# Three V steps to a block instead of two, in a kernel that mixes attention and a Fourier layer on one core

## The chip, the core and the metric

The kernel runs on one core of a Trainium2 chip. A core has a matrix engine (PE, with its weight loads shown apart as PEld), a vector engine (DVE), an activation engine (ACT), a general engine (POOL) and an engine that here issues all DMAs (SP). The engines run side by side, each through its own list of instructions in order, and wait for each other by semaphores. The metric is the device time of one execution in microseconds.

## What is computed

```python
x = A_x                                            # 2048 tokens, 640 wide
g = sigmoid((x * gate_w).sum(-1, keepdims=True))
a = x @ dft_hid_re.T ;  b = x @ dft_hid_im.T       # DFT along the width
y = dft_seq_re @ a - dft_seq_im @ b                # DFT along the sequence
q = x @ wq (32 heads of 20) ; k = x @ wk ; v = x @ wv   # one k and v for all heads
o = softmax(q k^T / sqrt(20)) v, heads side by side, @ wo
out = g * y + (1 - g) * o
```

All inputs are float32 and filled matrices; nothing uses that the DFT matrices are regular.

## The kernel before

After a first stage (q, k, v, gate) nearly the whole time goes to one long loop in which PE works on two things in turn.

**Attention.** Heads go in pairs. In one pair the two heads use the two halves of PE's rows (partitions 0 to 63 and 64 to 127), so that two matmuls run at once, one in each half. For each pair and each half of the queries (index v, 0 to 31) there are three kinds of unit:

- an `a` unit (`a_unit`, L243): scores of 128 queries against 512 keys, of which DVE takes the maximum (L258). After 64 of them for one v, `a_reduce` and `a_final` (L260, L265) form the 62nd and 61st row of that v's query tile `qs`: the negated maximum, as a high and a low part. They go out to `m_d` and back into `qs` by two DMAs each, put into the program one and five ticks later. There are four query tiles (L141).
- a `b` unit (`b_unit`, L944): scores of 128 keys against 512 queries with the maximum taken off, and on ACT the exponential, into a tile `pt` (16 of them, L582). Four `b` units are one step.
- a `V` step (`av_step`, L961): four products of `pt` with the values. Here the four column groups of PE work at once, each over all 128 rows. 16 steps end one v; then `finish_half` (L968) starts a chain of DMAs and a reciprocal (`finish_sums`) for the row sums.

There are 512 steps in all. The scores go to five PSUM banks, S0 to S4, each of which is free again when DVE or ACT has read it.

**Fourier layer.** It is cut into products of 64 rows by 128 columns with 320 columns of data, in float32 made of a high and a low part. `y_put` queues pairs of products, `y0` and `y1` run one in each row half (`Halves`, L758). They serve first the DFT along the width (stage AB, begun ahead of the loop), then 112 chunks of 24 pairs for the sequence (stage Y), then the output projection (`oo`). For each chunk POOL adds two input blocks where a product asks for it (L522), rounds to the high part `ch` (L527) and subtracts for the low part `cl` (L528). Two chunks end one group of sums: `y_evict` (the words `E0`, `E1`) lets ACT copy the two PSUM tiles and POOL add them (L809), and `y_out` adds them to earlier parts.

**The order.** PE, ACT, DVE and POOL run in the order of the program text; the order of the DMAs on SP is chosen by the framework's planner. The loop goes over 256 rounds (`ROUNDS`, L1064) of two steps. Each round has a plan, a list of words: `b0S1` is a b unit of row half 0 into bank S1, `a1S3` an a unit of row half 1, `y0`/`y1` a Fourier product, `V` a V step. All plans with `V` have two of them at their end, one behind the other:

```python
    AB15 = (   # 8 b, 8 a, 15 pairs y, E0 E1 V V     56 + 16 rounds
    Y16 = (    # 8 b, 8 a, 16 pairs y, E0 E1 V V     168 rounds, stage Y
    Y12 = (    # 8 b, 8 a, 12 pairs y, E0 E1 V V     while a units are left
    N12 = (    # 8 b, 12 pairs y, E0 E1 V V
    N0 =       # 8 b, V V                            last two rounds
```

(The comments stand for the words.) The V words of a round take the steps of the round before (`old`); the first round has no V steps, and four follow the last one (L1119). A chunk of 24 pairs takes one round and a half. `later` (L227) puts DMAs and small work into the program a number of ticks afterwards; two ticks pass with each step. Work of `chores` (`a_final`, `finish_sums`, `scale_kept`) goes to DVE's list at the next V.

**The end.** `load_last` (L701) is called after round 252 (counted from 0; the 13th of the 14 rounds of Y12 and N12): POOL clears two tiles, ten DMAs fill them, and three DVE instructions (`scale_kept`, L712) make operands of them. After the last V step `finish_last` (L990) copies its result half on ACT and half on DVE (L995, L996), takes the reciprocal of the sums and feeds the last projections (`o_group`).

Of the kernel before, what the change touches and what calls it, by code (L numbers as in the profile page):

```python
# [23 lines left out]
NT = S // P  # L24
NPAIR = H // 2
LAST = NPAIR - 1
HALF = D // 2
SJ = NT // 2
# [5 lines left out]
def kernel(  # L34
# [24 lines left out]
    def bank(tag, name):  # L59
        if tag in BANKS:  # L60
            turn[tag] += 1
            tag = BANKS[tag][(turn[tag] - 1) % len(BANKS[tag])]
        return psum.tile([P, ROW], F32, tag=tag, name=name, bufs=1)
# [49 lines left out]
    def move(dst, src):  # L113
        nc.sync.dma_start(words(dst), words(src))  # L114
# [112 lines left out]
    def later(n, f, *args):  # L227
        todo.append((clock["n"] + n, f, args))

    def tick():  # L230
        clock["n"] += 1
        due = [t for t in todo if t[0] <= clock["n"]]
        todo[:] = [t for t in todo if t[0] > clock["n"]]
        for _, f, args in due:
            f(*args)
# [48 lines left out]
    def do_chores():  # L284
        for q in (chores, act_chores):
            while q:
                f, *args = q.pop(0)
                f(*args)

    NA = NPAIR * 64  # L290
    state = [0, 0]

    def a_half(hh, tag="A"):
        u = state[hh]
        if u >= NA:
            return
        a_unit(u, hh, tag)
        state[hh] = u + 1
        if state[1 - hh] <= u:
            return  # L300
        v, r = divmod(u, UV)
        if r == 8 and v + 1 < 2 * NPAIR:
            load_qs(v + 1)
        if r == UV - 1:
            chores.append((a_reduce, v))
            chores.append((a_final, v))
            if not stage["loop"]:
                do_chores()
# [180 lines left out]
    def a_src(i, th):  # L489
        return lambda r, sh: (cre, cim)[i][SJ * th + r, sh]  # L490

    def s_src(k):
        return lambda r, sh: s_d[k][r, sh].rearrange("p (j t) -> p j t", j=SJ)

    PRODUCTS = (
        ("p1", (a_src(0, 0),), None, None, None),
        ("p2", (a_src(1, 0),), None, None, None),
        ("p5", (a_src(0, 1), a_src(1, 1)), ALU.add, 1, t_d[1]),
        ("p6", (s_src(1), a_src(0, 0)), ALU.subtract, 2, t_d[2]),
        ("p7", (a_src(0, 0), a_src(0, 1)), ALU.subtract, None, t_d[3]),  # L500
        ("p3", (a_src(1, 0), s_src(2)), ALU.subtract, None, b_d[1, 1]),
        ("p4", (a_src(1, 1),), None, None, t_d[4]),
    )
# [216 lines left out]
    def load_late():  # L720
        tb = NT - 1
        t = acc[tb] = abp.tile([P, 2, HALF], F32, tag=f"ab0{tb}", name="acc")
        move(t, y_d[tb * P : (tb + 1) * P].rearrange("p (e n) -> p e n", e=2))
        later(4, lambda: nc.gpsimd.tensor_scalar(t, t, gate[:, tb : tb + 1], None, op0=ALU.mult))
# [211 lines left out]
    def y_put(n):  # L936

        while n > 0:
            n -= next(ys)[1]
# [4 lines left out]
    def b_unit(p, hh, kc, qc, tag="B"):  # L944
        b = 64 * hh
        ps = bank(tag, f"b_{p}_{kc}_{qc}_{hh}")
        nc.tensor.matmul(  # L947
            ps,
            ks[b : b + 62, kc * P : (kc + 1) * P],
            qs[NPAIR * (qc // 2) + p][b : b + 62, (qc % 2) * ROW : (qc % 2 + 1) * ROW],  # L950
            start=True,
            stop=True,
        )
        t = pp.tile([P, ROW], F32, name="pt")
        nc.scalar.activation(t, ps, AF.Exp, scale=SCALE)  # L955
        pt[(hh, kc, qc)] = t

    def av_mm(ps, g, t, kc, first, last):
        nc.tensor.matmul(ps[32 * g : 32 * g + 32, :], vsb[:, kc, :], t, start=first, stop=last)  # L959

    def av_step(p, qh, kc):  # L961
        if kc == 0:
            av[qh] = bank("V", f"av_{p}_{qh}")
        for hh in range(2):
            for j in range(2):
                av_mm(av[qh], 2 * hh + j, pt.pop((hh, kc, 2 * qh + j)), kc, kc == 0, kc == NT - 1)

    def finish_half(p, qh):  # L968
        ob = op.tile([P, ROW], F32, name="ob")
        nc.scalar.activation(ob, av[qh], AF.Copy)  # L970

        sm = op.tile([P, 16], F32, name="sm")
        n = (1, 3, 5) if (p, qh) == (LAST - 1, 1) else (2, 6, 10)
        later(n[0], move, sum_d[p, qh].rearrange("h (j t) -> (h j) t", j=2), ob.rearrange("(g r) t -> g r t", r=32)[:, DH])
        for hh in range(2):
            h = 2 * p + hh
            for j in range(2):
                js = slice((2 * qh + j) * ROW, (2 * qh + j + 1) * ROW)
                g = 32 * (2 * hh + j)
                later(n[0], move, oT_d[h * DH : (h + 1) * DH, js], ob[g : g + DH])  # L980
        later(n[1], move, sm, sum_d[p, qh].rearrange("h (s t) -> (h s) t", t=16))
        later(n[2], chores.append, (finish_sums, p, qh, sm))
# [28 lines left out]
    def scale_rows(p, qh):  # L1011
# [11 lines left out]
    AB15 = (  # L1023
        "b0S1 a1S3 b1S2 y0 y0 a1S0 y0 y0 y1 y0 y1 y0 b1S4 y0 a1S1 y0 b0S3 y1 y1 y0 y1 a0S2 y1 y0 b1S0 y0 y1 "
        "a0S4 y1 b0S1 y1 y1 a0S3 y1 y0 y1 y0 y1 y0 y1 y0 y1 b0S0 b1S2 a0S4 a1S1 E0 E1 V V"
    ).split()

    Y16 = (
        "b0S1 a1S0 a0S3 b1S4 y0 y1 y0 y1 y0 y1 y0 y1 y0 b1S2 y0 a1S1 y0 y0 a1S0 y0 b1S4 y0 y0 y1 y0 b1S3 y0 y1 "
        "a0S2 y1 b0S1 y1 y1 y0 y1 y0 y1 b0S4 y1 a0S0 y1 y1 b0S3 y1 a0S2 y1 a1S1 y0 E0 E1 V V"  # L1030
    ).split()

    Y12 = (
        "b0S0 a1S3 a0S4 y1 y1 b0S1 y1 y0 b1S2 y1 y0 y0 a1S0 b0S3 y1 y0 y1 y0 a1S1 y0 y0 b1S4 y0 y1 y0 a1S2 "
        "b0S0 y0 y1 y1 a0S3 y1 b1S4 a0S1 y0 y1 y1 y0 b1S2 a0S0 E0 E1 V V"
    ).split()

    N12 = (
        "b0S4 b1S2 b0S3 b1S0 b1S1 y0 y0 y1 y0 y1 y0 y1 y0 y1 y0 y1 y0 y1 y0 y1 y0 y1 y0 y1 y0 y1 y0 y1 "
        "b0S2 y1 b0S3 b1S4 E0 E1 V V"  # L1040
    ).split()


    N0 = [w for w in N12 if w[0] not in "yE"]

    LEAD = 12
    NL = 2 * (UV + LEAD)
    KL = 15 * SJ
# [12 lines left out]
                y_evict(g)  # L1061
    stage["loop"] = True

    ROUNDS = [(p, qh, kk) for qh in range(2) for p in range(NPAIR) for kk in range(NT // 2)]  # L1064
    NAB = 7 * SJ
    NY = 3 * SJ * len(PRODUCTS)

    NO = len(ROUNDS) - NT * 2

    def plan_of(n):  # L1070
        if n < NAB or NO <= n < NO + NT:
            return AB15
        if n < NAB + NY:
            return Y16
        if n >= len(ROUNDS) - 2:
            return N0
        return Y12 if state[1] < NA else N12

    old = []

    for rnd in ROUNDS:
        p, qh, kk = rnd
        nb, fed = [0, 0], False
        new = [(p, qh, 2 * kk), (p, qh, 2 * kk + 1)]
        plan = plan_of(ROUNDS.index(rnd))
        puts = plan.count("y0")
        for what in plan:
            if what == "V":
                if old:
                    st = old.pop(0)  # L1090
                    av_step(*st)
                    do_chores()
                    if st[2] == NT - 1 and st[:2] != (LAST, 1):
                        finish_half(*st[:2])
                continue
            g = int(what[1])
            if what[0] == "y":
                if not fed:
                    y_put(puts)
                    fed = True  # L1100
                halves.run(g)
            elif what[0] == "E":
                y_evict(g)
            elif what[0] == "b":
                b_unit(p, g, 2 * kk + nb[g] // 2, 2 * qh + nb[g] % 2, what[2:])
                if sum(nb) % 2 == 0:
                    tick()
                nb[g] += 1
            else:
                a_half(g, what[2:])  # L1110
        old += new
        if (p, qh, kk) == (LAST, 1, 4):
            load_last()
        if (p, qh, kk) == (LAST, 1, 5):
            load_late()
    for g in range(2):
        y_evict(g)

    for st in old:  # L1119
        av_step(*st)  # L1120
    finish_last()
    for e in range(2):
        begin_late(e)
# [49 lines left out]
```

## Time and profile before

| | |
|---|---|
| device time, median of 3 runs | 1738.46 us (1738.17 to 1738.92) |
| the profiled execution | 1739.45 us, its span 1737.7 us |
| PE busy | 1715.7 us, 99% of the span |
| DVE, ACT, POOL busy | 79%, 73%, 63% |
| granted PE clock | 0.996 of full speed |
| matmul instructions | 16752, of them 4096 for V steps (eight to a step) |

A busy matrix engine is read with care: matmuls overlap one another, in each row half and at their ends, so 99% busy says that something was always under way, and not that it could not be denser. What one kind of work costs is read from the distance between starts, not from the duration of one instruction.

### The profile page before, as it was taken

The numbers are of one execution on the slowest core, as the hardware profiler recorded it, in microseconds if no ns is written. First come the engines' busy times: TensorE is split into PE (matmuls) and PEld (weight loads), VectorE is DVE, ScalarE is ACT, GpSimd is POOL, SyncE is SP. The second block draws the span as 40 slices with busy tenths as digits, with TensorE's granted clock in tenths as the row PEclk, the third lists the DMA queues.
The fourth block names the chain that finished last, engine by engine and source line by source line (L and its number), as shares of the span: only waits on it lengthen the run. The fifth ranks groups of instructions, "written<-read, shape, count | busy, mean of one in ns | idle before, by whom it ended". The sixth has DMA issues, their size and how long they took to land.

```text
span 1737.7 us, 43681 instructions
## 1 busy us (share of the span) xinstructions
PE 1715.7 (99%) x16752; PEld 1223.3 (70%) x16752; DVE 1369.1 (79%) x2290; ACT 1261.7 (73%) x2543; POOL 1102.2 (63%) x921
## 2 busy tenths in 40 slices
PE   8999999999999999999999999999999999999997
PEld 6687777777777777777777777777777777777664
DVE  4788888888888888888888888888888888888813
ACT  4237888888777777777777777777777767788895
POOL 3045556333366568668777888888877765557784
PEclk9999999999999999999999999999999999999999
DMA  8552223222265546546666777555555533244332
GB/s 264 158 165 63 71 81 102 78 72 74 78 213 171 176 157 188 185 128 227 225 204 214 222 253 220 185 179 185 183 163 170 159 114 100 76 124 116 104 94 78
DMA packets 181502, 261.50 MB, mean 150 GB/s; under 512 B 35696, under 2 KB 136304, under 8 KB 181292
## 3 DMA queue, kind: packets, MB, share of 16 engines
q1 hardware_dynamic: 181292, 258.70, 47.1%
q8 instruction: 132, 2.16, 0.5%
q14 instruction: 78, 0.64, 0.1%
HBM read 184.42 MB, written 76.99 MB: 150 GB/s over the span
## 4 chain that ended last, share of the span: by engine, by line
PE 94%; DVE 2%; DMA 2%; issue 1%; ACT 1%; POOL 0%; SPq 0%; POOLq 0%; ACTq 0%; DVEq 0%
PE av L959 27%; PE y_p L767 20%; PE b L947 19%; PE a L251 15%; PE ab L767 7%; PE oo L767 3%; PE q L122 1%; DVE mx L258 1%; PE q L123 1%; PE q L124 1%; DMA wraw<-in_wq_dram 1%; DMA wraw<-in_wiT_dram 0%; ACT pt L955 0%; SPq L114 0%; DVE xl L361 0%
## 5 line engine op out<-in xcount | busy, mean ns | idle before, releaser
L258 DVE TENSOR_REDUCE mx<-a 128x1 f32<-128x512 f32 x2048 | 1282.7, 685 | 263.2 <-PE a L251 245.0
L955 ACT ACTIVATE pt<-b 128x512 f32<-128x512 f32 x2048 | 1068.9, 606 | 342.1 <-PE a L251 287.2
L947 PE MATMUL b<-qs,ks 62*128 62x512 f32 x2048 | 749.9, 408 | 3.8 <-DVE mx L258 1.8
L251 PE MATMUL a<-ks,qs 60*128 60x512 f32 x2048 | 702.0, 408 | 2.2 <-DVE mx L258 2.2
L767 PE MATMUL y_p<-tb,ch 64*128 64x320 f32 x3584 | 627.3, 306 | 0.0
L947 PEld LDWEIGHTS b<-qs,ks 62*128 62x128 f32 x2048 | 342.8, 185 | 220.8 <-DVE mx L258 155.1
L959 PE MATMUL av<-pt,vsb 128*32 128x512 f32 x4096 | 492.3, 598 | 0.0
L767 PEld LDWEIGHTS y_p<-tb,ch 64*128 64x128 f32 x3584 | 476.2, 185 | 9.8
L767 PE MATMUL y_p<-tb,cl 64*128 64x320 f32 x1792 | 442.4, 306 | 0.0
L251 PEld LDWEIGHTS a<-ks,qs 60*128 60x128 f32 x2048 | 345.8, 185 | 8.2 <-issue 4.0
L767 PEld LDWEIGHTS y_p<-tb,cl 64*128 64x128 f32 x1792 | 271.2, 185 | 5.1
L528 POOL TENSOR_TENSOR cl<-craw,ch 128x1024 fp32r<-128x1024 f32 x112 | 268.3, 2395 | 9.0
L959 PEld LDWEIGHTS av<-pt,vsb 128*32 128x32 f32 x4096 | 106.9, 109 | 226.1 <-issue 216.9
L809 POOL TENSOR_TENSOR yt<-yt,yu 128x320 f32<-128x320 f32 x86 | 74.9, 871 | 299.1 <-ACT yu L804 267.1
L809 POOL TENSOR_TENSOR abt<-abt,abu 128x320 f32<-128x320 f32 x64 | 55.7, 871 | 194.1 <-ACT abu L804 186.3
L522 POOL TENSOR_TENSOR craw<-craw 128x1024 f32<-128x1024 f32 x64 | 153.7, 2401 | 0.0
L527 POOL CAST ch<-craw 128x1024 fp32r<-128x1024 f32 x112 | 116.4, 1039 | 6.4 <-PE ab L767 2.3
L767 PE MATMUL oo<-wo,osp 64*128 64x320 f32 x816 | 92.6, 306 | 0.0
L767 PEld LDWEIGHTS oo<-wo,osp 64*128 64x128 f32 x816 | 87.4, 185 | 1.6
L554 POOL TENSOR_TENSOR tb<-braw,tb 128x320 fp32r<-128x320 f32 x80 | 68.5, 879 | 0.0
L767 PE MATMUL ab<-wbh,xh 64*128 64x320 f32 x256 | 60.1, 307 | 0.0
L767 PE MATMUL ab<-wbh,xl 64*128 64x320 f32 x256 | 59.8, 305 | 0.0
(138 smaller groups left out, 1626.9 us busy)
## 6 DMA issues: line engine op xcount, KB each, us to landing
craw<-in_cre_dram SPq DMA_DIRECT2D x80, 512.0 KB
craw<-in_cim_dram SPq DMA_DIRECT2D x64, 512.0 KB
s_d<-craw SPq DMA_DIRECT2D x32, 512.0 KB
craw<-s_d SPq DMA_DIRECT2D x32, 512.0 KB
braw<-b_d SPq DMA_DIRECT2D x80, 160.0 KB
xraw<-in_xT_dram SPq DMA_DIRECT2D x32, 320.0 KB
b_d<-abt SPq DMA_DIRECT2D x64, 160.0 KB
t_d<-braw SPq DMA_DIRECT2D x64, 160.0 KB
```

The lines of the kernel that those rows point to most:

```text
L122: nc.tensor.matmul(ps, wh, xh, start=(i == 0), stop=False)
L251: nc.tensor.matmul(ps, qs[v][b : b + 60, qb * P : (qb + 1) * P], ks[b : b + 60, c * ROW : (c + 1) * ROW], start=True, stop=True,)
L258: nc.vector.tensor_reduce(mx[v][:, hh, qb, c : c + 1], ps, axis=AX.X, op=ALU.max)
L522: nc.gpsimd.tensor_tensor(raw[0], raw[0], raw[1], op=how)
L527: nc.gpsimd.tensor_copy(h, raw[0])
L528: nc.gpsimd.tensor_tensor(l, raw[0], h.bitcast(F32), op=ALU.subtract)
L554: nc.gpsimd.tensor_tensor(t[:, 1], raw, t[:, 0].bitcast(F32), op=ALU.subtract)
L767: nc.tensor.matmul(ps, w, x, start=start, stop=stop)
L809: nc.gpsimd.tensor_tensor(t0, t0, t1, op=ALU.add)
L947: nc.tensor.matmul(ps, ks[b : b + 62, kc * P : (kc + 1) * P], qs[NPAIR * (qc // 2) + p][b : b + 62, (qc % 2) * ROW : (qc % 2 + 1) * ROW], ...
L955: nc.scalar.activation(t, ps, AF.Exp, scale=SCALE)
L959: nc.tensor.matmul(ps[32 * g : 32 * g + 32, :], vsb[:, kc, :], t, start=first, stop=last)
```

## The change

A plan Y24 is added: 12 b units, 12 a units, 24 pairs of products, E0 E1 and three V steps. In stage Y the 168 rounds of Y16 give way to seven cycles of 18 plans: each cycle has 12 of Y24, in couples, and 6 of Y16, in threes, so that a couple of Y24 (48 pairs) and three Y16 (48 pairs) each end one group of sums. The V words take steps from a list to which the plan's own steps are added before its words are run, so that V runs one step behind the newest one, and no longer two to four. The first plan, FIRST, has four more b units (one more step) and two V steps. The last two plans are N0 and a short one with four b units and two V steps, and no V steps follow the loop. `load_last` and `load_late` are called by the number of steps made. The other plans have the same words as before.

```diff
+    Y24 = (
+        "b1S0 a0S2 b1S4 y0 y0 a1S1 y0 y1 y0 b1S3 y0 y0 y1 y0 y1 a0S0 b1S2 y0 y1 y0 b1S4 y0 a1S1 y0 y0 y1 b0S3 y1 "
+        "y1 y0 a1S0 y0 b0S2 y1 y0 y1 y1 b0S4 a1S1 y0 y0 y1 y0 y1 y1 b0S3 y1 a0S0 y1 b0S2 y1 y1 y0 y1 a0S4 b1S1 y0 "
+        "y1 y0 y1 y0 y1 y0 y1 y0 y1 b0S2 a1S0 a0S3 y1 a1S4 a0S1 E0 E1 V V V"
+    ).split()
+
+    FIRST = AB15[:-2] + "b0S3 b1S0 b0S2 b1S3 V V".split()
...
-    ROUNDS = [(p, qh, kk) for qh in range(2) for p in range(NPAIR) for kk in range(NT // 2)]
+    STEPS = [(p, qh, kc) for qh in range(2) for p in range(NPAIR) for kc in range(NT)]
...
+    CYCLE = []
+    for k in range(8):
+        CYCLE += [Y16] * 3 if k in (2, 5) else [Y24] * 2
+
+    def plans():
+        yield FIRST
+        yield from [AB15] * (NAB - 1)
+        for _ in range(7):
+            yield from CYCLE
+        yield from [AB15] * NT
+        for _ in range(NT - 2):
+            yield Y12 if state[1] < NA else N12
+        yield N0
+        yield N0[:4] + N0[-2:]
...
-    for rnd in ROUNDS:
-        p, qh, kk = rnd
+    for plan in plans():
+        n = sum(w[0] == "b" for w in plan) // 4
+        new = STEPS[made : made + n]
+        made += n
+        old += new
...
             if what == "V":
-                if old:
-                    st = old.pop(0)
-                    av_step(*st)
-                    do_chores()
...
+                st = old.pop(0)
+                av_step(*st)
+                do_chores()
...
-        old += new
-        if (p, qh, kk) == (LAST, 1, 4):
+        if made == len(STEPS) - 5:
             load_last()
-        if (p, qh, kk) == (LAST, 1, 5):
+        if made == len(STEPS) - 3:
             load_late()
...
-    for st in old:
-        av_step(*st)
     finish_last()
```

More of the change, by code (lines that the diff above doesn't have):

```diff
@@ L1062 @@
     stage["loop"] = True
-    ROUNDS = [(p, qh, kk) for qh in range(2) for p in range(NPAIR) for kk in range(NT // 2)]
+    STEPS = [(p, qh, kc) for qh in range(2) for p in range(NPAIR) for kc in range(NT)]
     NAB = 7 * SJ
[L1066 to L1077, printed above, removed]
-    old = []
-    for rnd in ROUNDS:
-        p, qh, kk = rnd
+    CYCLE = []
[11 more added lines that the diff above has]
+        yield N0[:4] + N0[-2:]
+    made = 0
+    old = []
+    for plan in plans():
[3 more added lines that the diff above has]
+        old += new
         nb, fed = [0, 0], False
-        new = [(p, qh, 2 * kk), (p, qh, 2 * kk + 1)]
-        plan = plan_of(ROUNDS.index(rnd))
         puts = plan.count("y0")
@@ L1088 @@
             if what == "V":
-                if old:
-                    st = old.pop(0)
-                    av_step(*st)
-                    do_chores()
-                    if st[2] == NT - 1 and st[:2] != (LAST, 1):
-                        finish_half(*st[:2])
+                st = old.pop(0)
+                av_step(*st)
+                do_chores()
+                if st[2] == NT - 1 and st[:2] != (LAST, 1):
+                    finish_half(*st[:2])
                 continue
@@ L1104 @@
             elif what[0] == "b":
-                b_unit(p, g, 2 * kk + nb[g] // 2, 2 * qh + nb[g] % 2, what[2:])
+                p, qh, kc = new[nb[g] // 2]
+                b_unit(p, g, kc, 2 * qh + nb[g] % 2, what[2:])
                 if sum(nb) % 2 == 0:
@@ L1110 @@
                 a_half(g, what[2:])
-        old += new
-        if (p, qh, kk) == (LAST, 1, 4):
+        if made == len(STEPS) - 5:
             load_last()
-        if (p, qh, kk) == (LAST, 1, 5):
+        if made == len(STEPS) - 3:
             load_late()
+    assert made == len(STEPS) and not old
     for g in range(2):
         y_evict(g)
-    for st in old:
-        av_step(*st)
     finish_last()
```

## The prediction

> **What bounds the kernel now.** I read the busy line of the page first, then the chain that ended last, then the costliest groups.
>
> ```profile
> PE 1715.7 (99%) x16752; PEld 1223.3 (70%) x16752; DVE 1369.1 (79%) x2290; ACT 1261.7 (73%) x2543; POOL 1102.2 (63%) x921
> PE 94%; DVE 2%; DMA 2%; issue 1%; ACT 1%; POOL 0%; SPq 0%; POOLq 0%; ACTq 0%; DVEq 0%
> L258 DVE TENSOR_REDUCE mx<-a 128x1 f32<-128x512 f32 x2048 | 1282.7, 685 | 263.2 <-PE a L251 245.0
> L955 ACT ACTIVATE pt<-b 128x512 f32<-128x512 f32 x2048 | 1068.9, 606 | 342.1 <-PE a L251 287.2
> L767 PE MATMUL y_p<-tb,cl 64*128 64x320 f32 x1792 | 442.4, 306 | 0.0
> ```
>
> PE makes 94% of the chain, and before the products of stage Y it never stands idle (0.0). DVE and ACT wait for PE in their main groups. So only what shortens PE's own sequence counts. The timeline of PE shows that sequence; its columns are start, duration, instruction and count. The V blocks that close stage AB and stage Y, one round late in stage Y, and the last V block, which has four steps:
>
> ```profile
> 475.03 1.92 PE L959 MATMUL av<-pt,vsb 128*32 128x512 f32 x16
> 1529.30 1.06 PE L959 MATMUL av<-pt,vsb 128*32 128x512 f32 x8
> ...
> 1328.55 1.92 PE L959 MATMUL av<-pt,vsb 128*32 128x512 f32 x16
> 1330.40 0.50 PE L947 MATMUL b<-qs,ks 62*128 62x512 f32 x1
> 1330.74 0.39 PE L947 MATMUL b<-qs,ks 62*128 62x512 f32 x1
> 1330.97 0.31 PE L767 MATMUL y_p<-tb,ch 64*128 64x320 f32 x2
> ...
> 1710.14 3.64 PE L959 MATMUL av<-pt,vsb 128*32 128x512 f32 x32
> ```
>
> From 475.03 to 1529.30 lie the 168 rounds of Y16; they take 1054.27 us, **6.275** each (the row at 1529.30 is cut by its window; its start counts). Two V steps last 1.92 and four 3.64, so one more step in the same block costs (3.64 - 1.92) / 2 = **0.86**. After a V block the first b follows 1.85 behind the V start, 0.13 more than two steps. The second unit of a row half comes 0.34 behind the first, but the next 0.23 behind that: a unit of 512 columns takes 0.235 and the first one 0.10 more. The chain of waits gives the pair of products:
>
> ```profile
> 1699.15 1.61 PE oo L767 x22
> ```
>
> Eleven pairs in 1.61 are **0.147** a pair. A Y16 round in each row half has 8 units of a or b and 16 products: 8 x 0.235 + 16 x 0.147 = 4.23, with 1.72 for V 5.95. The round takes 6.275, so **0.33** of each round is the two changes of mode: 0.13 from V to rows, 0.10 at the first unit, the rest (0.10) before V.
>
> **The change part by part.**
>
> *Fewer blocks.* Per step nothing is added in stage Y: Y24 has 12 a, 12 b, 24 pairs and 3 V, one and a half times Y16. The 168 blocks become 7 x 18 = 126, so 42 changes of mode go: 42 x 0.33 = **-13.9 us**. The exponentials, maxima, POOL operations and DMAs are as many as before.
>
> *The order inside Y24.* Walking the words with 0.235 and 0.147, each row half on its own would need 0.34 + 11 x 0.235 + 24 x 0.147. The records of PE stand in the timeline in the order of the words; so a word that starts no earlier than the one ahead of it holds up its half. At the fourth y0 (half 0 ready at 0.78, y1 ahead of it at 0.81), and twice later, a half is held 0.03 to 0.04; at the end 0.05 remain. The trace has no Y24, so I bound this by two plans, worked out as Y16 less the pairs that they lack:
>
> ```profile
> 142.56 1.92 PE L959 MATMUL av<-pt,vsb 128*32 128x512 f32 x16
> ...
> 1651.83 1.92 PE L959 MATMUL av<-pt,vsb 128*32 128x512 f32 x16
> 1657.88 1.50 PE L959 MATMUL av<-pt,vsb 128*32 128x512 f32 x12
> ```
>
> AB15 takes (475.03 - 142.56) / 54 = 6.157, and 6.275 - 0.147 = 6.128 would be due: 0.03 lost. Y12 takes 6.05 against 5.69: 0.36 lost, part of it waits for banks. Per Y24 that is 0 to 0.5; I take the walk's 0.05, beside AB15, whose share of a and b units is almost the same. 84 x 0.05 = **+4.2 us**. A Y24 block comes to 1.5 x 6.275 - 0.165 + 0.05 = **9.30**. The Trainium skill, "TensorE: Matmul & The Clock Gate", Part 3, The mechanism, says that matmuls start and end strictly in program order, even where they use different rows; by it the 4.2 stand, and without it the change would gain them.
>
> *Cover.* Timeline of PE:
>
> ```profile
> 805.95 0.40 PE L947 MATMUL b<-qs,ks 62*128 62x512 f32 x1
> ...
> 807.66 1.92 PE L959 MATMUL av<-pt,vsb 128*32 128x512 f32 x16
> ```
>
> DVE needs 12 x 0.63 = 7.5 and ACT 12 x 0.52 = 6.3 of 9.30 (the busy times above by 2048), so both keep up; the walk leaves each bank about the 0.2 us that Y16 leaves it. The V words now take fresh steps. In Y16 the second V needs the sixth b (805.95), 1.7 before the block and 2.6 before its own start, four exponentials of time; Y24's third V needs the ninth of twelve and starts 1.7 into the block. I cost the waits at nothing. POOL in the product with most additions:
>
> ```profile
> 1002.12 1.48 PE L959 MATMUL av<-pt,vsb 128*32 128x512 f32 x9
> 1003.28 0.87 POOL L809 TENSOR_TENSOR yt<-yt,yu 128x320 f32<-128x320 f32 x1 [2.46 <-ACT yu L804]
> ...
> 1009.61 2.39 POOL L528 TENSOR_TENSOR cl<-craw,ch 128x1024 fp32r<-128x1024 f32 x1
> ```
>
> The second chunk's `cl` is ready 9.9 behind the V that ends a group. Two Y24 need it 9.30 + 2.71 + 0.34 = 12.3 behind; POOL's cover grows.
>
> *The head.* FIRST brings a V block and four b units forward; the round 0 of before had no V.
>
> ```profile
> 136.50 0.40 PE L251 MATMUL a<-ks,qs 60*128 60x512 f32 x2
> 138.28 0.49 PE L947 MATMUL b<-qs,ks 62*128 62x512 f32 x1 [1.38 <-DVE mx L258]
> ...
> 137.98 0.46 ACT L804 ACTIVATE abu<-ab 128x320 f32<-128x320 f32 x1
> ```
>
> The four new b follow at 136.74. The last of them needs bank S3 a second time; its exponential queues behind the eviction at 137.98, so runs from 138.3 to 138.9, and V starts at 138.9 + 0.33 = 139.3. The second plan then reaches its V at 139.3 + 6.16 = 145.4 instead of 142.56: **+2.9** (+0.9 if nothing waited, +3.5 if the last maximum at 138.2 came first).
>
> *The tail.* V block and b units that moved to the head are missing here. Timelines of PE, POOL, ACT and DVE:
>
> ```profile
> 1705.53 1.92 PE L959 MATMUL av<-pt,vsb 128*32 128x512 f32 x16
> ...
> 1708.08 4.03 ACT L955 ACTIVATE pt<-b 128x512 f32<-128x512 f32 x8 [0.59 <-PE b L947]
> 1713.87 0.38 ACT L995 ACTIVATE ob<-av 128x256 f32<-128x256 f32 x1 [1.77 <-PE av L959]
> ...
> 1703.11 1.85 POOL L705 MEMSET oraw<- 128x1024 f32 x2
> ...
> 1712.73 1.23 DVE L718 TENSOR_TENSOR osp<-oraw,osp 128x1024 fp32r<-128x1024 f32 x1
> ...
> 1714.29 0.42 DVE L996 COPY ob<-av 128x256 f32<-128x256 f32 x1 [0.34 <-ACT ob L995]
> ```
>
> After V at 1705.53 only four b would follow; their exponentials end at 1708.08 + 3 x 0.48 + 0.6 = 1710.1, the last V step ends about 1.5 behind that, 2.3 before 1713.87. But `finish_last` needs DVE, and `scale_kept` ends there at 1713.96. It hangs on POOL's clearing (1703.11) and ten DMAs behind it, which stand at the same plan as before and do not move. DVE's copy could come forward from 1714.29 to 1714.0 and no further: **-0.3**. This chain, hidden now, becomes the bound of the tail. If it also moved, -2.3.
>
> *Sum:* -13.9 + 4.2 + 2.9 - 0.3 = **-7.1**. From the profiled execution (1739.45) this gives 1732.35; it is 0.99 above the median of the runs, so 1731.4 against 1738.46.
>
> **The rivals.**
>
> *A new wait: the maximum rows of `qs`.* b units now run one step earlier, and `a_final` waits for the end of a longer plan. Timelines of DVE, SP and PE, the worst case first, then the best in stage Y:
>
> ```profile
> 1309.71 1.92 PE L959 MATMUL av<-pt,vsb 128*32 128x512 f32 x16
> ...
> 1311.84 0.22 DVE L273 TENSOR_REDUCE m<-m 128x32 fp32r<-128x64 f32 x1
> ...
> 1321.04 1.22 SPq L114 DMA_DIRECT2D m_d<-m  x2
> ...
> 1325.51 0.55 SPq L114 DMA_DIRECT2D qs<-m_d  x2
> ...
> 606.79 1.50 PE L959 MATMUL av<-pt,vsb 128*32 128x512 f32 x12
> ...
> 609.29 1.21 SPq L114 DMA_DIRECT2D m_d<-m  x2
> ...
> 612.77 0.55 SPq L114 DMA_DIRECT2D qs<-m_d  x2
> ```
>
> `a_final` is done 2.35 behind its V start, the first b that needs it comes at 1330.40, 20.7 behind. The load is issued 6.5 (best) to 16.35 (worst) behind, since SP stands in other waits; it needs some 2.3 more (as `m_d`: 610.50 to 612.77). In the change, counting words, the first such b is 10.8 behind the V start for 7 of the 21 tiles of stage Y (from the second Y24 of a couple into the second Y16) and 13.8 for 14. The 7 tight ones stand at the end of a group, as 606.79 does, where SP has little to wait for: ready at 6.5 + 0.7 (Y24 ends with four a, so one more maximum lies ahead of `a_final`) + 2.3 = 9.5, 1.3 to spare. If SP there stands behind the next `cl` (9.9), the load lands at 9.9 + 0.6 + 2.3 = 12.8, 2.0 late, 7 x 2.0 = 14; seven others, in the middle of a group, may wait for `cl` of the following chunk and be about 0.6 late, 4 more. That gives 1731.4 + 18 = **1749**, slower. It decides from 10.6 us on, 0.5 per tile. For it: every one of these DMAs goes through SP in order. Against it: the reciprocal's DMAs, which hold SP in the worst cases, come 9 to 18 ahead of `a_final` now instead of 6.
>
> *The order costs nothing, or the tail's chain moves too.* -4.2 or -2.0 more: **1726**.
>
> *The change does less than it says*: single tiles are late, or Y24 loses 0.1 as Y12 does in part (84 x 0.05 more = 4.2), or both: about **1737**, no change that can be told.
>
> **How the numbers follow.** The forecast (1727 to 1735) has 0.60, the better case 0.13, the middle one 0.13, the new wait 0.14. A measurement of this kernel can tell about 0.2% from no change, 3.5 us. Faster is forecast and better case, 0.73; same 0.13; slower 0.14. The range: below, the better case with the smaller head, 1725; above, a good part of the new wait, 1744. The end of Y12's bound (84 x 0.5 = 42) lies outside; its bank waits have no place in the walk.
>
> **What would show it.** Right: 126 V blocks in stage Y, 84 of 24 records with 9.25 to 9.35 from one such V start to the next, Y16 at 6.275; the first V near 139.3; DVE's copy right behind `scale_kept`, with ACT's copy done 2 us earlier. Wrong: idle time of PE before the first b of a v, released by DMA `qs<-m_d`; PE waits for S0 to S4 inside Y24; idle before products from POOL `cl`; Y24 above 9.4.

## The result and the profile after: slower by 1.6%, with the gain in place

| | before | after |
|---|---|---|
| median of four runs each | 1738.32 us (1735.83 to 1738.92) | 1765.43 us (1762.49 to 1768.61) |
| ratio, with its 95% interval | | 1.0159 (1.0136 to 1.0182) |
| the profiled execution, its span | 1739.45, 1737.7 us | 1763.66, 1761.8 us |
| mean granted PE clock | 0.996 | 0.992 |

The forecast of 1731.4 us was wrong, and wrong in sign. The first rival, a wait for the maximum rows of `qs`, came true, and cost more than it was priced at. The page of after (busy line, chain by engine, the group of b units with its mean duration and the idle time ahead of it), then the view of waits for PE in stage Y (us in total, times, longest):

```profile
PE 1719.1 (98%) x16752; PEld 1245.2 (71%) x16752; DVE 1387.3 (79%) x2290; ACT 1252.9 (71%) x2543; POOL 1100.8 (62%) x921
PE 85%; DMA 4%; POOL 4%; issue 3%; DVE 2%; SPq 1%; ACT 1%; POOLq 0%; DVEq 0%; ACTq 0%
L947 PE MATMUL b<-qs,ks 62*128 62x512 f32 x2048 | 759.6, 410 | 22.8 <-DMA qs<-m_d 20.4
...
PE b L947 <- DMA qs<-m_d: 20.4, 10, 3.9
```

PE's share of the chain fell from 94% to 85%; DMA, POOL and issue have taken its place. That is one kind of wait with what lies ahead of it: ten times in stage Y PE stands before the first b unit of a tile until its rows have landed. The view shows nothing else for which PE waits in stage Y.

The timeline of PE gives the stages. First two V starts with nothing between that waits, then the V that closes stage AB and the one that closes stage Y:

```profile
486.57 2.78 PE L959 MATMUL av<-pt,vsb 128*32 128x512 f32 x24
495.89 2.78 PE L959 MATMUL av<-pt,vsb 128*32 128x512 f32 x24
...
478.09 1.92 PE L959 MATMUL av<-pt,vsb 128*32 128x512 f32 x16
1554.76 2.78 PE L959 MATMUL av<-pt,vsb 128*32 128x512 f32 x24
```

A Y24 takes 9.32 here, and 9.31 elsewhere. Without waits the stage would be 84 x 9.31 + 42 x 6.275 = 1045.6, 8.7 less than the 1054.27 of before. It took 1554.76 - 478.09 = 1076.67. So **31.1 us** went into waits, of which only 20.4 are idle time. Most of the rest is the clock: the trace's records of the granted clock have five stretches of 0.5 in stage Y, 20.5 us together, each at or behind one of the five longest waits (2.15 us and more). At half speed they cost some 9 to 10 us (an estimate: half of 20.5, less what was idle anyhow). The span's 24.1 us divide into +3.06 up to the end of stage AB (478.09 against 475.03), +22.4 in stage Y (-8.7 and +31.1) and -1.4 behind it.

One wait in full, from the timelines of PE, DVE and SP and from the table of stretches (length, busy time of each engine, granted clock, DMA share, GB/s):

```profile
968.22 2.78 PE L959 MATMUL av<-pt,vsb 128*32 128x512 f32 x24
975.35 1.92 PE L959 MATMUL av<-pt,vsb 128*32 128x512 f32 x16
983.20 0.76 PE L947 MATMUL b<-qs,ks 62*128 62x512 f32 x1 [3.94 <-DMA qs<-m_d]
987.94 2.15 PE L959 MATMUL av<-pt,vsb 128*32 128x512 f32 x16
...
971.00 0.22 DVE L273 TENSOR_REDUCE m<-m 128x32 fp32r<-128x64 f32 x1
...
974.76 1.29 SPq L114 DMA_DIRECT2D m_d<-m  x2
978.35 0.55 SPq L114 DMA_DIRECT2D qs<-m_d  x2
...
981.00:985.00 4.00, 1.80 (x12) 1.83 (x14) 0.00 (x0) 0.85 (x2) 3.86 (x4) 0.58 0.95 324
985.00:988.00 3.00, 3.00 (x24) 2.51 (x25) 1.62 (x3) 2.20 (x5) 0.40 (x1) 0.50 0.82 273
```

The maximum is there at 971.2, 3.0 behind the V start. SP sends it out only at 974.76, sends for the way back at 978.35, and the rows land at 983.20, 4.3 behind the end of that issue, while the DMA engines are 95% busy (981 to 985). The block from 975.35 to 987.94 is a Y16; it takes 12.59 instead of 6.275, **6.3 lost for 3.94 of waiting**: the clock falls to half and stays there into the work that follows. What held SP from 968 to 980 stands in its view of waits, of which these are the two longest rows:

```profile
SPq L114 <- POOL part L594: 3.8, 2, 3.3
SPq L114 <- POOL craw L522: 2.0, 1, 2.0
```

The DMAs ahead of the maximum on SP's list store results that POOL had not finished. It is not always POOL: before the rows of the tile that waits 2.59 us, whose V starts at 1072.87, SP stood 4.4 us for the landing of the reciprocal's `rec_d<-rc`.

### The profile page after: what moved, and what is told of

It reads as the page before. It is cut to its first block, busy times and chain, and to the rows that moved or that the text cites. A ratio compares the mean times of both kernels' runs of the same rounds, so it can differ in the third digit from the quotient of the medians.

```text
span 1761.8 us, 43342 instructions
## 1 busy us (share of the span) xinstructions
PE 1719.1 (98%) x16752; PEld 1245.2 (71%) x16752; DVE 1387.3 (79%) x2290; ACT 1252.9 (71%) x2543; POOL 1100.8 (62%) x921
## 4 chain that ended last, share of the span: by engine, by line
PE 85%; DMA 4%; POOL 4%; issue 3%; DVE 2%; SPq 1%; ACT 1%; POOLq 0%; DVEq 0%; ACTq 0%
PE av L959 24%; PE y_p L767 18%; PE b L947 17%; PE a L251 13%; PE ab L767 6%; PE oo L767 3%; DMA qs<-m_d 2%; DVE mx L258 1%; PE q L122 1%; PE q L123 1%; POOL cl L528 1%; PE q L124 1%; DMA m_d<-m 1%; POOL craw L522 1%; POOL ch L527 1%
## 5 line engine op out<-in xcount | busy, mean ns | idle before, releaser
L258 DVE TENSOR_REDUCE mx<-a 128x1 f32<-128x512 f32 x2048 | 1302.8, 685 | 271.2 <-PE a L251 228.9
L947 PE MATMUL b<-qs,ks 62*128 62x512 f32 x2048 | 759.6, 410 | 22.8 <-DMA qs<-m_d 20.4
L251 PE MATMUL a<-ks,qs 60*128 60x512 f32 x2048 | 711.1, 409 | 2.4 <-DVE mx L258 2.2
L767 PEld LDWEIGHTS y_p<-tb,ch 64*128 64x128 f32 x3584 | 510.1, 187 | 2.7
L947 PEld LDWEIGHTS b<-qs,ks 62*128 62x128 f32 x2048 | 347.8, 186 | 207.8 <-DVE mx L258 115.1
L959 PE MATMUL av<-pt,vsb 128*32 128x512 f32 x4096 | 485.9, 598 | 0.0
L767 PE MATMUL y_p<-tb,cl 64*128 64x320 f32 x1792 | 458.4, 308 | 0.0
L767 PEld LDWEIGHTS y_p<-tb,cl 64*128 64x128 f32 x1792 | 299.1, 187 | 3.1
L959 PEld LDWEIGHTS av<-pt,vsb 128*32 128x32 f32 x4096 | 111.5, 109 | 241.8 <-issue 232.1
```

The costliest lines, as they stand in the source:

```text
L251: nc.tensor.matmul(ps, qs[v][b : b + 60, qb * P : (qb + 1) * P], ks[b : b + 60, c * ROW : (c + 1) * ROW], start=True, stop=True,)
L258: nc.vector.tensor_reduce(mx[v][:, hh, qb, c : c + 1], ps, axis=AX.X, op=ALU.max)
L767: nc.tensor.matmul(ps, w, x, start=start, stop=stop)
L947: nc.tensor.matmul(ps, ks[b : b + 62, kc * P : (kc + 1) * P], qs[NPAIR * (qc // 2) + p][b : b + 62, (qc % 2) * ROW : (qc % 2 + 1) * ROW], ...
```

## The experiments

My theory after this reading: the rows come as late as they did before (SP takes its DMAs in order), but b and the maximum have moved towards each other. Over the 21 tiles of stage Y the way back is issued 10.4 us behind the V start (median), where it was 11.2 in the kernel before. Rivals: the DMA path itself got worse through the bigger blocks; or V steps on fresh exponentials are at fault and the wait for the rows only shows where they are made up. In all experiments, where nothing else is said, the kernel is the changed one with one edit. Ratios are to the kernel before on the same chip.

### More distance: LEAD 16, and the opposite in the kernel before

`LEAD` is the number of a units that each row half is ahead when the loop begins. The kernel before gets 8 in the same line.

```diff
-    LEAD = 12
+    LEAD = 16
```

> The changed kernel with the a units 16 instead of 12 ahead (four per row half earlier, two steps). Theory (the b units wait for the maximum rows of qs, because they come only 11 to 16 us behind the V block at which a_final runs): the first b comes some 6.3 us later behind it, 17 to 22 us; all ten waits for DMA qs<-m_d go, stage Y falls by about 32 us, and the time is 1728 to 1737 us. Rival (Y24 itself, its banks or the DMA load of the longer blocks make the loss): the lead changes nothing in stage Y, the time stays at 1755 us or more.

> The kernel before, V blocks of two, with the a units 8 instead of 12 ahead, so that the first b of a v comes 14.4 us behind its V block instead of 20.7. Theory (distance alone makes the loss): with the issue times of before (6.5 to 16.4 us) and 2 to 3 us to land, five to nine tiles are late by 0.5 to 4 us, and the time rises by 10 to 30 us, to 1750 to 1770. Rival (the waits come with Y24): no waits for qs<-m_d, 1735 to 1743 us.

LEAD 16: 1739.99 us, ratio 1.0021 (1.0011 to 1.0030). LEAD 8 in the kernel before: 1747.4 us, ratio 1.0059 (1.0044 to 1.0074). The waits for the rows, LEAD 16 first:

```profile
PE b L947 <- DMA qs<-m_d: 2.6, 1, 2.6
```

```profile
PE b L947 <- DMA qs<-m_d: 8.7, 3, 4.6
```

Nine of ten waits are gone with more lead, and the kernel before gets the same wait when its lead is cut. So the distance decides, and neither Y24 nor the fresh V steps. With LEAD 8 three tiles were late, where I had expected five to nine, and the time stayed under my 1750 to 1770. LEAD 16 came out above what I expected, because the lead has a price of its own (below).

### Later b units, V steps with them

```diff
-    FIRST = AB15[:-2] + "b0S3 b1S0 b0S2 b1S3 V V".split()
+    FIRST = AB15[:-1]
...
-        yield N0[:4] + N0[-2:]
+        yield N0 + ["V"]
```

(`load_last` and `load_late` one step earlier as well.)

> The changed kernel whose first plan is AB15 with one V step and no additional b units, and whose last plan is N0 with three V steps: the blocks of three V steps and all plans between stay, but the b units run one step later than in the change. Theory (distance of the b units from a_final): each first b of a v comes 3.1 us later, 14 to 19 us behind its V block; of the ten waits (20.4 us of idle PE) at most three stay with some 3 us together, the clock drops go, and the time is 1728 to 1738 us. Rival (the blocks of three themselves): no change, 1755 us or more.

1764.18 us, ratio 1.0155 (1.0140 to 1.0170): no gain, but the loss has another name.

```profile
PE av L959 <- ACT ob L970: 27.8, 31, 2.0
```

There is no wait for `qs<-m_d` in this run, so one step more (3.1 us) was enough here, with these pauses beside it. But all V steps also moved by one, so that the last step of one v and the first of the next fall into the same V block, and the one PSUM bank of the V steps has to be copied by ACT in between, 31 times at 0.9 us. In the changed kernel the cycle 3,3,3,3,2,2 | 2,3,3,3,3,2 | 2,2,3,3,3,3 ends every v at the end of a block. That had been in no row I had read.

### Where in the plan the maximum is complete

`a_final` goes to DVE at a V. With LEAD 12 the last a units of the three tiles of a cycle fall at steps 10, 26 and 42 of its 48; the plans end at 12, 27 and 42. So `a_final` runs 3, 4 and 5 steps ahead of the step that uses the tile. I call them kinds one, two and three. Taken in the order of the words, the first b unit of a tile, one of row half 1, comes 10.85, 13.90 and 13.88 us behind the V start where nothing waits (V starts 1442.61, 1489.36 and 1536.14): in kind three that unit stands early in its Y24. (The 11.2, 14.3 and 16.0 us of the second expectation below are those of another b unit, every 64th in order of time, and that need not be the first of its tile.)

```diff
-    LEAD = 12
+    LEAD = 14
```

> LEAD = 14 instead of 12: every a unit stands one step (3.1 us) earlier. Theory: a_final is run only at a V, so what counts is at which plan's end the last a unit of a tile falls. With LEAD 12 it falls ten steps into a cycle, in the fourth Y24, which ends at step 12 (tiles v8, v11, v14, v17, v20, v23); one step earlier it falls at the end of the third Y24, so a_final comes a whole plan, 9.3 us, earlier, and these six waits (13.0 us of idle time, 20 us of lost time with the clock) go; the other two kinds of tile end in the same plan as before, and their four waits stay (7.4 us idle, 12 us lost). Head and end together cost 1 to 2 us. 1745 to 1751 us. Rival: the steady distance alone counts, each tile gains 3.1 us, nearly all ten waits go: about 1735 us.

And a cycle of 8 Y24 and 12 Y16 in which plans end at 10, 26 and 42, with LEAD 12:

```diff
-        CYCLE += [Y16] * 3 if k in (2, 5) else [Y24] * 2
+        CYCLE += [Y24] * 2 if k in (0, 3, 6, 7) else [Y16] * 3
```

> Another cycle with LEAD 12: two Y24, six Y16, two Y24, six Y16, four Y24 (8 of Y24 and 12 of Y16 in place of 12 and 6), so that the last a unit of every tile falls at the end of a plan, and the first b unit of every tile comes five steps behind (nominally 16.0 us instead of 11.2, 14.3 and 16.0). Theory: the eight waits of the first two kinds go, at most the two of the third kind stay (2 to 4 us idle); stage Y is 84 x 6.275 + 56 x 9.31 = 1048.5, 2.9 us longer than without waits. 1735 to 1743 us. Rival: not the distance but the DMA traffic of three V blocks' worth of products holds the rows up; then about as many waits as now, 1760 us or more.

LEAD 14 gave 1743.71 us, ratio 1.0033 (1.0019 to 1.0046); the other cycle 1747.65, ratio 1.0055 (1.0038 to 1.0072). The waits, LEAD 14 first:

```profile
PE b L947 <- DMA qs<-m_d: 4.6, 3, 1.9
```

```profile
PE b L947 <- DMA qs<-m_d: 7.6, 3, 3.7
```

With LEAD 14 exactly the six waits of kind one went; of the other four three stayed, two of kind two and one of kind three. So a lead of one step more gives nothing to a tile whose last a unit stays in the same plan, and a whole plan (9.3 us) to one where it passes a plan's end. The time was a little under my 1745 to 1751. The other cycle brought the 14 tiles of kinds one and two to 16.3 us; those of kind three stayed at 13.9. Three waits stayed, one of kind three; I had expected 1735 to 1743 and at most two waits, of kind three alone. Two are of what was kind two; there SP sent the maximum out only 11.8 and 12.0 us behind the V start. So 16 us is not enough everywhere either; with the 20.7 of before the same lateness was hidden.

The third wait with LEAD 14 shows what such a wait costs. Timeline of PE and a stretch of that run:

```profile
1070.74 2.78 PE L959 MATMUL av<-pt,vsb 128*32 128x512 f32 x24
1077.38 0.47 PE L947 MATMUL b<-qs,ks 62*128 62x512 f32 x1 [1.87 <-DMA qs<-m_d]
1083.67 2.78 PE L959 MATMUL av<-pt,vsb 128*32 128x512 f32 x24
...
1077.00:1081.00 4.00, 3.62 (x29) 3.65 (x31) 2.07 (x3) 2.29 (x5) 1.61 (x2) 0.69 0.65 225
```

The block took 12.93 instead of 9.31, 3.6 lost for 1.87. In the changed kernel shorter waits cost themselves and 0.3 more; timeline of PE:

```profile
673.24 1.92 PE L959 MATMUL av<-pt,vsb 128*32 128x512 f32 x16
678.63 0.47 PE L947 MATMUL b<-qs,ks 62*128 62x512 f32 x1 [1.48 <-DMA qs<-m_d]
681.25 1.92 PE L959 MATMUL av<-pt,vsb 128*32 128x512 f32 x16
```

8.01 instead of 6.275 is 1.74 for 1.48, at full clock. The Trainium skill, "TensorE: Matmul & The Clock Gate", Part 1, What's actually happening, has the clock fall to half after at least one idle window of about 3.4 us. By that rule the wait of 1.87 us should have cost no clock; the stretch behind it shows 0.69, so the measurement decides. But the length of a wait alone does not tell what it costs. Here are the stretches behind two waits of like length, 2.15 us (it ended at 1302.39 in the changed kernel) and 2.18 us (1305.99 in the run with the earlier `load_last`, below):

```profile
1302.40:1305.80 3.40, 3.40 (x22) 3.40 (x24) 0.69 (x1) 1.97 (x4) 3.08 (x2) 0.51 0.05 12
...
1306.00:1309.40 3.40, 3.40 (x36) 2.63 (x40) 1.99 (x4) 2.90 (x6) 3.07 (x2) 1.00 0.08 11
```

The first halved the clock, the second did not. In the clock records of the changed kernel the half-clock stretches of stage Y begin at 981.62, 1039.65, 1090.85, 1148.87 and 1302.47, whole multiples of 3.413 us apart, and each lasts once or twice that. The wait of 2.15 us lies between two such marks; the one of 2.18 us, by the marks of its own run, was cut at 1305.05 into 1.24 and 0.94. So it seems to be the idle time between two marks that counts; no run tested that, and a limit in us cannot be read from these runs.

### A shorter way for the rows: three attempts

The DMAs of the rows issued by ACT in place of SP; only the way out issued by ACT (the first of the two edits alone); and POOL's own stores issued by POOL, to free SP of the waits ahead of the rows.

```diff
+    def move_a(dst, src):
+        nc.scalar.dma_start(words(dst), words(src))
...
-            later(1, move, m_d[v][i].rearrange("r g t -> g r t"), m3[:, 1 + i])
+            later(1, move_a, m_d[v][i].rearrange("r g t -> g r t"), m3[:, 1 + i])
...
-            later(5, move, qs[v][r : r + 2], m_d[v][:, hh * QB : (hh + 1) * QB].rearrange("i b g t -> i (b g t)"))
+            later(3, move_a, qs[v][r : r + 2], m_d[v][:, hh * QB : (hh + 1) * QB].rearrange("i b g t -> i (b g t)"))
```

```diff
+    def move_p(dst, src):
+        nc.gpsimd.dma_start(words(dst), words(src))
...
-                later(4, move, s_d[save][k // 2, k % 2].rearrange("p (j t) -> p j t", j=SJ), raw[0])
+                later(4, move_p, s_d[save][k // 2, k % 2].rearrange("p (j t) -> p j t", j=SJ), raw[0])
...
-            move(t_d[z][k], t)
+            move_p(t_d[z][k], t)
...
-            later(8, move, part_d[k][r], t)
+            later(8, move_p, part_d[k][r], t)
```

> The changed kernel with the four DMAs of the maximum rows (two m_d<-m, two qs<-m_d for each v) issued from ACT, the load three ticks behind instead of five; nothing else moves. Theory that the rows are late because they stand in SP's queue behind waits for POOL and for other DMAs: m_d is issued about 3.3 us behind the V start instead of 3 to 10, the rows are there by about 9, most of the waits go, 1730 to 1742 us. Rival that the landing itself is slow (the load lands 2 to 5 us after its issue while the DMA engines are full) or that ACT's stops cost as much: waits of 1 us and more stay on the seven tight tiles, 1745 us or more.

> Only the way out (m_d<-m) is issued by ACT, the way back (qs<-m_d) stays on SP. Theory: part of the lateness is SP's queue; in the ten waits m_d left 4.6 to 10 us behind the V start though the maximum was there at 3.0. Issued by ACT at about 3.5 it lands by 7 to 8, and the way back need not wait for it: idle time before b falls from 20 us to 5 to 10, ACT loses some 1.3 us at the start of 21 plans, partly hidden: 1745 to 1756 us. Rival: SP issues the way back as late as before for other reasons, or ACT's exponentials become late: no gain, 1760 to 1775 us.

> LEAD 12 and the cycle as in the changed kernel; the stores of POOL's own results (t_d<-braw, s_d<-craw, part_d) are issued by POOL itself and no longer by SP, which so far stood in wait for POOL at each of them with m_d and qs behind it. Theory: the rows are late because SP takes its DMAs in order; then m_d goes out at 3.1 to 5 behind the V start instead of 5 to 10, qs is issued by 7 to 9 and there by 9 to 12, and of the ten waits at most three of the first kind of tile stay: 1733 to 1745 us. Rival: issuing costs POOL more than it spares (some 130 DMAs), cl comes late and products wait: 1760 us or more.

1834.61 us (ratio 1.0566, 1.0548 to 1.0583), 1811.07 (1.0431, 1.0409 to 1.0454) and 1797.68 (1.0350, 1.0336 to 1.0364): all three much worse, the second above even the 1760 to 1775 of its rival. PE's waits with both ways on ACT (lines here are three higher than in the changed kernel), and ACT's timeline at one way back:

```profile
PE b L950 <- ACT pt L958: 40.6, 31, 5.8
...
527.51 4.25 ACTq L117 DMA_DIRECT2D qs<-m_d  x2
531.87 1.57 ACT L958 ACTIVATE pt<-b 128x512 f32<-128x512 f32 x3 [3.79 <-DMA t_d<-braw]
```

Here the two issues of the way back took 4.25 us, where SP takes 0.55, and ACT's next exponential came only behind them. What the issue waited for is not shown. With only the way out on ACT, waits of PE and the timelines of ACT and SP behind the V that starts at 996.98:

```profile
PE b L950 <- ACT pt L958: 26.5, 23, 6.9
PE b L950 <- DMA qs<-m_d: 24.6, 9, 4.3
...
1000.36 1.15 ACTq L117 DMA_DIRECT2D m_d<-m  x2
...
1008.61 0.55 SPq L114 DMA_DIRECT2D qs<-m_d  x2
```

The maximum leaves 3.4 behind the V start, as expected, and SP sends for it only at 11.6. So the way back was late on SP's list although the maximum had left early. With POOL's stores on POOL, waits of PE and SP, the group of one kind of store, and a V start with the way out behind it:

```profile
PE b L950 <- DMA qs<-m_d: 46.0, 14, 7.1
...
SPq L114 <- POOL cl L531: 193.1, 62, 8.2
...
SPq L114 <- DMA t_d<-braw: 60.9, 18, 6.4
...
L117 POOL DMA_DIRECT2D t_d<-braw x64 | 34.7, 549 | 0.0
...
994.94 2.78 PE L962 MATMUL av<-pt,vsb 128*32 128x512 f32 x24
1001.49 1.21 SPq L114 DMA_DIRECT2D m_d<-m  x2
```

An issue costs POOL 0.55 us, and SP now waits for the same stores to land before it may load them, and longer for `cl` (193.1 us in all, 171.9 in the changed kernel). My expectation of an early `m_d` fell: for this tile, the one of 968.22 above, it leaves 6.55 behind the V start, as late as with the stores on SP (974.76 - 968.22 = 6.54). So SP's lateness isn't those stores alone. What else makes it up in each tile was not taken apart, and an earlier place in the program for the way back on SP itself was not tried. The Trainium skill, "DMA: Bandwidth & Descriptors", Issuing engines are not separate DMA queues, says that issuing from several engines at once saves only the time that it takes to initiate the DMAs. These runs gained nothing by it: they lost 61 to 98 us against the kernel before, where the unaltered change lost 27.

### The end

```diff
-        if made == len(STEPS) - 5:
+        if made == len(STEPS) - 7:
             load_last()
```

> load_last one plan earlier (at 7 steps before the end instead of 5); everything else as in the changed kernel. The chain POOL clearing, ten DMAs, scale_kept, DVE's copy of ob stood 2.1 us behind ACT's copy; if it was the bound of the end, DVE's copy now follows ACT's: 1.5 to 2.3 us less, 1763 us, and the wait of the sums falls from 2.64 to about 0.5. Rival: the DMAs wait for something else as well (rows of oT_d or rec_d that come late), no gain.

1763.97 us, ratio 1.0158 (1.0137 to 1.0179): no difference that the runs can tell. The trace shows the mechanism. Timelines of after, then of this run:

```profile
1732.17 1.92 PE L959 MATMUL av<-pt,vsb 128*32 128x512 f32 x16
1740.53 1.12 PE L998 MATMUL sums<-ob,spread 128*128 128x512 f32 x2 [2.64 <-DVE ob L996]
...
1738.91 1.22 DVE L718 TENSOR_TENSOR osp<-oraw,osp 128x1024 fp32r<-128x1024 f32 x1
1740.06 0.41 DVE L996 COPY ob<-av 128x256 f32<-128x256 f32 x1
...
1737.93 0.38 ACT L995 ACTIVATE ob<-av 128x256 f32<-128x256 f32 x1 [1.14 <-PE av L959]
```

```profile
1740.52 0.42 DVE L996 COPY ob<-av 128x256 f32<-128x256 f32 x1 [3.52 <-ACT ob L995]
...
1740.99 1.12 PE L998 MATMUL sums<-ob,spread 128*128 128x512 f32 x2 [0.93 <-DVE ob L996]
```

After: DVE's copy follows `scale_kept` without a gap, 2.1 behind ACT's. Earlier loads: it follows ACT's, and the wait of the sums falls from 2.64 to 0.93. 1.7 us are too few beside stalls that vary by as much from run to run.

### Together, and the price of the lead

LEAD 16 and LEAD 18, both with the earlier `load_last`; and LEAD 16 in the kernel before, which has nothing to gain from it.

> The kernel before with LEAD = 16: the price of the lead by itself. No wait for qs to remove there, so only the head (4.6 us longer, eight maxima of 0.57 on DVE) and the stages behind Y (1.6 shorter, fewer a units) should show: 1740 to 1742 us. Rival: the lead costs nothing by itself, then the changed kernel with LEAD = 16 (1740) contained a loss of 7 us in stage Y that is not yet explained: 1737 to 1738 us here.

> The changed kernel with LEAD = 16 and load_last one plan earlier: both earlier findings together. From 1740 us the end gives back 1.1 to 1.7 us; the one wait at about 1079 us (third kind of tile, 2.6 us idle, 4.3 lost) stays. 1738 to 1739.5 us.

> The same with LEAD = 18: the last a unit of the third kind of tile (v10, v13, v16, v19, v22) then falls at the end of the plan before, so that its rows start 9.3 us earlier and the wait at 1079 us goes as well; no PE wait for qs is left in stage Y (sum of what exceeds the steady periods under 1.5 us). The lead costs 2.3 us more in the head and gives 0.8 back behind stage Y. 1735 to 1737.5 us. Rival: with so much lead another limit shows (query tiles, maxima), waits of DVE or PE for qs<-qh_d: 1740 us or more.

| | us | ratio |
|---|---|---|
| kernel before, LEAD 16 | 1739.75 | 1.0020 (1.0011 to 1.0029) |
| changed, LEAD 16, earlier loads | 1739.30 | 1.0013 (1.0004 to 1.0021) |
| changed, LEAD 18, earlier loads | 1736.25 | 0.9997 (0.9988 to 1.0006) |

Both runs of the changed kernel lie inside what I had expected; the kernel before lies 0.25 us below its range.

With LEAD 18 no wait of PE is left between 480 and 1540 us. The group of b units, and the V starts that close stage AB and stage Y:

```profile
L947 PE MATMUL b<-qs,ks 62*128 62x512 f32 x2048 | 753.8, 408 | 2.4 <-ACT pt L955 1.4
...
485.62 1.92 PE L959 MATMUL av<-pt,vsb 128*32 128x512 f32 x16
1531.35 2.78 PE L959 MATMUL av<-pt,vsb 128*32 128x512 f32 x24
```

Stage Y takes 1045.73, **8.5 less** than before: the saving is real. The next two runs give the same, 1045.67 with the change and 1054.27 without. But stage AB closes 10.6 later than before, 7.5 of it by the lead. DVE's timeline shows where, kernel before first, then LEAD 18:

```profile
118.28 15.03 DVE L258 TENSOR_REDUCE mx<-a 128x1 f32<-128x512 f32 x25
```

```profile
117.40 22.20 DVE L258 TENSOR_REDUCE mx<-a 128x1 f32<-128x512 f32 x37
```

Twelve more maxima in a row, without a gap between them, at 0.6 each; fewer a units behind stage Y give a part back. The kernel before pays 3.4 us for LEAD 16 by itself. So the change with its waits removed brings nothing here, because the longer head, most of it the price of the lead, takes about what stage Y saves.

### Ten of the maxima earlier

In the trace with LEAD 18 DVE is idle 1.3 to 1.4 us before four of the last five splits of a q tile, 0.3 before the other. Two a units go into each of these five steps of the q projection:

```diff
                 for c in range(KC):
                     q_mm(ps, n, m, c)
+                    if (n, c) == (3, 2):
+                        for z in range(2):
+                            a_half(z, f"S{1 + z}")
```

> The changed kernel with LEAD = 18 and the earlier load_last, and ten a units put into the projections ahead of the loop (two in each of five steps of q, where DVE stood idle 1.3 us per step by the trace of the run before): the loop's start is no longer behind 12 additional maxima. If the lead costs DVE time in the head, 10 x 0.57 = 5.7 us go and 10 x 0.12 to 0.24 of PE come in their place: 3.3 to 4.5 us less, 1731.7 to 1733 us, first V near 142. Rival: the projections are held up by the maxima or their banks as much as the head was: 1736 us or more.

> The kernel before with the same ten a units in the projections, LEAD = 12: the placement by itself. The head is as much shorter as above if DVE bounds it there too (3.3 to 4.5 us: 1732 to 1733 us), and then what the change is worth with all its waits gone is the difference to the run above, 0 to 1 us; rival: with LEAD = 12 the head is bound by the Fourier products on PE and not by DVE, 1735 to 1737 us.

Changed kernel with LEAD 18, earlier loads and this: **1734.65 us, ratio 0.9987 (0.9978 to 0.9995)**; the kernel before with this alone: 1736.75, ratio 0.9998 (0.9989 to 1.0007). The first is the only version faster than the kernel before, by 0.13%, some 2.3 us where 7.1 were forecast for the change alone. Against the second, which has the early units too, the change with its lead and the earlier loads is worth 2.1 us, where I had expected 0 to 1. The gain over the run without the early units is some 1.7 us by the two ratios, half or less of the 3.3 to 4.5 that I expected; in the kernel before the early units gained nothing that can be told, as the rival of that run had it. DVE's timeline without, then with them:

```profile
103.81 0.69 DVE L373 TENSOR_TENSOR ql<-q,qh 128x512 fp32r<-128x512 f32 x1 [1.28 <-ACT qh L372]
```

```profile
108.78 0.69 DVE L373 TENSOR_TENSOR ql<-q,qh 128x512 fp32r<-128x512 f32 x1 [0.71 <-ACT qh L372]
```

The last q tile is split 5.0 us later. Of this 0.7 were there before the first of the ten units (the sixth split from the end starts at 79.58 against 78.90), so the ten cost the projections 0.43 each. That is two to four times the 0.12 to 0.24 at which I had costed them, and three quarters of the 0.57 that they spare. Whether PE's time or a PSUM bank sets that price was not tried.

## Why the prediction failed, point by point

- **Fewer blocks, and the order inside Y24** (-13.9 and +4.2): right in their sum, which is all that the runs show; they do not part the two. Y24 takes 9.31 where 9.30 was forecast, Y16 its 6.275, and the stage without waits 1045.6 to 1045.7 where 1044.6 was due.
- **The head** (+2.9): right, +3.06; the first V came at 139.65, forecast 139.3.
- **The tail** (-0.3): the mechanism was right, the hidden chain became the bound. DVE's copy stands 7.89 behind the row of the last but one V where it stood 8.76 (1714.29 - 1705.53): -0.87. The whole stretch behind stage Y gave -1.4; where the other 0.5 comes from was not looked into.
- These terms come to 3.06 - 8.7 - 1.4 = -7.0, against the -7.1 of the sum. **What failed is the step "ready at 6.5 + 0.7 (...) + 2.3 = 9.5, 1.3 to spare"**, by which the wait for the rows of `qs` got no term in the sum and the rival only 18 us: +31.1 where 0 stood. In six of the seven tiles for which it was written the rows were there only 11.7 to 15.0 us behind the V start, and the first b unit was due at 10.85. The sentence "I cost the waits at nothing" was written of banks and of V steps on fresh exponentials, and for those it held: PE waited for neither in stage Y.
- **Why the rival was given too little.** First, "ready at 9.5, 1.3 to spare" took the best of the traced tiles as typical. In the trace of before the loads of the 21 tiles of stage Y are issued 6.5 to 16.35 behind the V start, with a median of 11.2; the two rows that I quoted are the ends of that spread. With 2.3 for the landing the median tile is ready at 13.5, past the 10.8 that I had counted. Second, the landing: 2.3 came from a quiet stretch (DMA share 0.24 from 609 to 613 us), and the row above shows 4.3 beside DMA engines that are 95% busy. The distances were not at fault: 10.8 and 13.8 were counted, 10.85 and 13.9 came, and of the seven tight tiles six waited, of the 14 others four. Third, the price: five of the ten waits also halved the clock, which makes up most of the step from 20.4 us of idle time to 31.1.
- **"Against it: the reciprocal's DMAs come 9 to 18 ahead"** took one holder of SP for the one that counts. In the worst case that I had quoted (1309.7 to 1326) SP stood 7.3 us for POOL's `cl` and not for the reciprocal. In the changed kernel, of the ten tiles that waited, it stood longest for POOL's results in six, for the landing of the reciprocal's DMA in two (4.4 and 3.8 us) and for that of other stores in two.

The experiments show that it is the distance (LEAD up and down, in both kernels), that it goes by the plan in which the last a unit falls (LEAD 14), and that the saving of the change stays when the waits are gone (LEAD 18). That the slow landing comes from the big transfers beside it was read from the DMA share and not tested by itself. Open too is which of SP's waits would have to go for the rows to come early: the three attempts at it only made other waits longer.

## What to carry to other kernels

When a change brings a consumer nearer to a transfer, take the whole spread of "ready" times from the trace, set it against each new distance, and count the tail, not the best row. A transfer that stands in an in-order queue behind another engine's results can be as late as that engine. Work that is only run at the end of a block moves in whole blocks: a small shift gives nothing or a full period.

## What had not been expected of the hardware

- A wait of 1.87 us dropped PE's granted clock for the work that followed (0.69 in the stretch behind 1077.38), and one of 3.94 us did (0.58 and 0.50 in the stretches around 983.20); one of 1.48 us did not, nor did one of 2.18 us (1.00 behind 1305.99). The loss was up to 2.4 us on top of the wait.
- A DMA of two rows of 1024 elements landed 4.3 us behind its issue beside 0.95 of DMA share.
- A DMA issued by POOL occupied it for 0.55 us.
